# Gated linear attention feeding a two-layer MLP: time order inside the chunks, and scores by halves in two column tiles

## The chip, the cores and the metric

The kernel runs on one core of a Trainium2 chip. The time is the device time of one execution in microseconds. The kernel before was run three times: 701.5, 701.19 and 699.17 us, a median of 701.19.

## What is computed

An attention block with complex decays (a running state per head, and no softmax) is followed by an MLP with a squared ReLU. B is 4, H 8, S 768 and D 48, all in f32; the MLP is 384 x 2048 x 384 over 3072 tokens.

```python
mag = sqrt(a_re**2 + a_im**2)
a = (a_re + 1j*a_im) * minimum(mag, 0.999) / (mag + 1e-6)
for t in range(S):                       # state: complex D x D for each batch and head
    state = a[t][:, None] * state + outer(k[t], v[t])
    y[t] = q[t] @ real(state)
x = y.transpose(0, 2, 1, 3).reshape(B*S, H*D)      # 3072 x 384
out = maximum(x @ w_in, 0)**2 @ w_out              # 384 -> 2048 -> 384
```

## The kernel before

**Units.** The work is cut into 6 units of 512 time steps (rows of the 3072 tokens). A unit is 4 chunks of 128 steps. The 8 heads form two halves z of 4 heads and four pairs i of two heads; pairs 0 and 1 belong to z = 0. The decays become a running product P, so that y = (q P) against (k / P): with the real and imaginary parts side by side, a head's queries and keys are 96 long, and inside a chunk the output is the masked product of scores with v, plus what the state from earlier chunks gives.

**Steps of a unit.** `load` brings a, q, k and v. `chain` normalises the decays on ACT and DVE, multiplies them up (`inner`, over 4 neighbouring steps; `totals` and `scan` over the rest, with PE transposes of `xn` there and `back` again), and `apply` makes the queries and keys: L1156 and L1160 are the products and sums with the running product, L1167 to L1179 the inverse, L1190 the products with q and k. `gather` (L1226) copies the keys by DMA from `f` into `KC`, where partitions are time. Then come the pairs:

- `turn` (units 2 to 5) brings queries and keys into `QT`, with partitions over the 96: two 32 x 32 block transposes of DVE (L1262) and 12 DMAs. `turn_pe` (units 0 and 1) does it by 16 PE transposes a pair (L1285) and 4 ACT copies (L1289).
- `score` (L1303), once per head: keys against queries for 4 chunks, 128 x 128 each, into a PSUM bank `sc`. DVE multiplies the bank by the causal mask (L1306) into `A`, which stands in SBUF.
- `keep` (L1331): keys against v, which DVE adds up into the states after each chunk (L1340, L1342, in `St` and `S`).
- `mix`: for each chunk and both heads v against `A` (L1355), and the state against the queries (L1359), into `yp`; the first head lands on partitions 0 to 47, the second on 64 to 111. ACT copies `yp` to `yt` (L1365), and DMAs bring it to `xT` (L1373), the MLP's input.

`dense` is the MLP, twice a unit on 256 rows: the first layer (L1395), ReLU and square on ACT (L1426, L1427), and the second: plain in unit 0 (L1441), and in units 1 to 5 by blocks of 128 x 192 (L1492), mostly 7 products in place of 8, with sums on DVE (L1507, L1516). Early in the kernel DVE also converts the weights to the layouts that the MLP reads (`convert`, L812 to L819).

**Who sets the order.** Every step is recorded in a `Plan` with its engine, an estimated duration, the keys that it reads and writes, and a rank. `Plan.order` then plays the program through: it takes the engine that can start soonest and gives it the ready step of the lowest rank. The instructions are written out in that order, and each engine runs its own in order, waiting by semaphores. On PE a step with `slack=True` that is fed by DMA is placed as if its input came 2.0 us later, any other that another engine feeds 0.6 later. `Plan.order` walks a Python set of engine names, so ties can fall differently from one build to the next: the profiled build and the rows printed here differ in units 0 and 1 in this way, with the same instructions.

**Where time lies.** Inside a chunk, time step 4t + c stands at partition 32c + t: `v`, `KC`, the columns of `QT`, the scores and the mask are in this order, and the copy L1365 puts the time back in order, writing to `yt` with elements 16 bytes apart. Sums of complex products are one operation on both parts, for which the imaginary factor is kept a second time with its sign changed (`minus`, L1044, and a third plane of `e`, `el`).

Of the kernel before, what the change touches and what calls it, by code (L numbers as in the profile page):

```python
# [598 lines left out]
def fast_path(ctx, tc, q, k, v, a_re, a_im, moe_w_in, moe_w_out, out, flag):  # L599
# [38 lines left out]
    def sb(name, n, dtype=F32, rows=C):  # L638
        return const.tile([rows, n], dtype, name=name)
# [33 lines left out]
    mask = sb("mask", C)  # L673
# [12 lines left out]
            for n in ("d0", "d1", "d2", "sc0", "sc1", "tr0", "tr1", "yp")}  # L686
# [40 lines left out]
    SUM = 0.22  # L727
    checked = []
# [28 lines left out]
    def two(t):  # L757
# [9 lines left out]
    tkeys = [[("QT", 2)], [("QT", 2), ("A", 2)], [("v", 1)]]  # L767
# [4 lines left out]
            (QT[0].bitcast(U32)[:, 0:2 * PW], [("QT", 0)]),  # L772
            (QT[1].bitcast(U32)[:, 0:2 * PW], [("QT", 1)]),
# [81 lines left out]

    def load(n):
# [23 lines left out]
        for i in range(W):  # L880
            b, s = divmod(n * L + i * C, S)
            src = v[b, :, s:s + C, :].rearrange("h (t c) d -> c t h d", c=W)
            for c in range(W):
                vrank = (CHAIN, 1) if n == 1 else (DENSE, 6 + n)
                dma(pool, [("xT", (n - (vs(n) == vs(n - 1))) % 2, NM - 1)] if n else [("gate",)], [("v", vs(n))],
                    lambda i=i, c=c, src=src: pool.dma_start(  # L886
                        out=t[32 * c:32 * c + 32, i], in_=src[c]), vrank, 32 * 1536, 4.0,
                    group=n)

    def chain(n):  # L890
# [57 lines left out]
        def inner(z):  # L948
# [4 lines left out]

            for c in range(1, W):
# [6 lines left out]
                for r, op in ((0, ALU.subtract), (1, ALU.add)):  # L961
                    step("DVE", tt(m // 2), [("in", z, 0), ("in", z, 1)] + key(z, 0), [("a", z)],
                         lambda c=c, r=r, op=op: dve.tensor_tensor(  # L963
                             out=a[:, r, :, c], in0=f[0][:, r], in1=f[1][:, 1 - r], op=op), ahead)
            xh = xn.rearrange("p r (h d) -> p r h d", h=H)[:, :, ts(z, HH)]
            step("ACT", ac(Z // W), [("a", z)], [("xn", 0, z), ("xn", 1, z)],
                 lambda: act.copy(out=xh[:, 0:2], in_=a[:, :, :, W - 1]), ahead)  # L967
# [716 lines left out]
```

## Time and profile before

| | |
|---|---|
| median of 3 runs (lowest, highest) | 701.19 us (699.17, 701.5) |
| the profiled execution | 698.23 us |
| its span, from the first to the last instruction | 696.4 us |
| granted TensorE clock over the span | 0.998 |
| PE busy, matmul instructions | 625.9 us, 4058 |
| DVE, ACT, POOL busy | 545.3, 351.5, 178.0 us |
| moved by DMA | 79.51 MB |

The span is one execution under the hardware profiler, and the profiled execution's time is 1.8 us longer than it. PE is the matrix engine, PEld its weight loads, DVE, ACT and POOL the vector, scalar and GpSimd engines, SP an engine that issues DMAs; an engine's row with a q behind its name is its queue. A row of a group reads: line, engine, operation, out <- in (partitions x elements), count | busy us, mean ns of one | idle us before it, and what ended it. An f32 matmul instruction of a 128 x 128 weight shows up as two passes on PE, so passes are counted in the timeline and source instructions in the order. The lengths in PE's rows overlap, and some passes are missing from the records.

### The profile page before, as it was taken

To read this page: it belongs to the slowest core of one execution; us is meant where nothing else is said; L and a number is where in the kernel's file an instruction comes from. 1 tells how busy PE (TensorE), PEld (TensorE's weight loads), DVE (VectorE), ACT (ScalarE), POOL (GpSimd) and SP (SyncE) were. 2 spreads that over 40 slices of the span, in tenths; PEclk is the share of its full clock that TensorE was granted. 3 is DMA by queue.
4 is the path that set the end of the run, shared out by engine and by line. 5 is a ranking of instruction groups with operands and counts; after the bars stand their busy time and mean duration, and the time that the engine had idled before them with its cause. 6 is when DMAs were issued, how large, how long until landed. Compare 5 with 4: busy or idle time off the path is not lost.

```text
span 696.4 us, 11428 instructions
## 1 busy us (share of the span) xinstructions
PE 625.9 (90%) x4058; PEld 563.6 (81%) x4058; DVE 545.3 (78%) x1111; ACT 351.5 (50%) x580; POOL 178.0 (26%) x334
## 2 busy tenths in 40 slices
PE   0115999999979999999999999999999999999996
PEld 0004887686768999998999998989999989989995
DVE  6999994889897699486898796999788988338631
ACT  6687738865864254346453437363456361142230
POOL 6604461143300005105036041043050033023100
PEclk9999999999999999999999999999999999999999
DMA  9751469021630005644018571027560025368600
GB/s 282 233 208 45 113 138 295 9 61 36 167 106 12 12 13 132 172 114 129 13 38 213 139 158 34 1 69 200 130 163 10 24 72 130 95 243 298 229 2 27
DMA packets 56354, 79.51 MB, mean 114 GB/s; under 512 B 10944, under 2 KB 38464, under 8 KB 56288
## 3 DMA queue, kind: packets, MB, share of 16 engines
q0 software_dynamic: 15232, 40.72, 19.2%
q1 hardware_dynamic: 36928, 32.98, 18.4%
q10 hardware_dynamic: 4128, 4.98, 2.8%
q8 instruction: 34, 0.56, 0.4%
q14 instruction: 32, 0.26, 0.1%
HBM read 48.76 MB, written 4.72 MB: 77 GB/s over the span
## 4 chain that ended last, share of the span: by engine, by line
PE 83%; DVE 11%; DMA 2%; issue 1%; SPq 1%; ACT 1%; DVEq 0%; ACTq 0%
PE d L1395 33%; PE d L1492 27%; PE d L1441 6%; PE sc L1303 5%; PE tr L1331 3%; PE yp L1355 3%; PE yp L1359 2%; PE tr L1395 1%; PE sc L1395 1%; DVE f L957 1%; DMA aq<-in_a_im_dram 1%; DVE f L1190 1%; PE tr L985 1%; DVE f L1156 1%; DVE aq L963 1%
## 5 line engine op out<-in xcount | busy, mean ns | idle before, releaser
L1395 PE MATMUL d<-xT,w 128*128 128x256 f32 x1056 | 233.6, 380 | 0.4 <-DMA xT<-yt 0.4
L1395 PEld LDWEIGHTS d<-xT,w 128*128 128x128 f32 x1056 | 199.1, 190 | 27.8 <-issue 1.2
L1492 PE MATMUL d<-w,g 128*128 128x192 f32 x832 | 143.3, 327 | 0.0
L1492 PEld LDWEIGHTS d<-w,g 128*128 128x128 f32 x832 | 135.5, 190 | 0.7 <-issue 0.4
L1426 ACT ACTIVATE g<-d 128x512 f32<-128x512 f32 x88 | 52.5, 596 | 117.0 <-PE d L1395 103.3
L1226 POOL DMA_DIRECT2D KC<-f x160 | 78.9, 501 | 93.7 <-DVE f L1190 49.5
L1453 POOL DMA_DIRECT2D out_dram<-ot x22 | 12.4, 565 | 268.4 <-DVE ot L1516 228.1
L1427 ACT ACTIVATE g<-g 128x512 f32<-128x512 f32 x96 | 60.6, 631 | 3.1
L1365 ACT COPY yt<-yp 112x512 f32<-112x512 f32 x24 | 26.3, 1095 | 70.0 <-PE yp L1359 70.0
L886 POOL DMA_DIRECT2D v<-in_v_dram x80 | 47.8, 605 | 50.2 <-issue 36.5
L1507 DVE TENSOR_TENSOR g<-g 128x512 f32<-128x512 f32 x56 | 37.8, 685 | 28.7 <-ACT g L1427 21.3
L1492 PE MATMUL d<-T,g 128*128 128x192 f32 x336 | 59.9, 327 | 0.0
L1492 PEld LDWEIGHTS d<-T,g 128*128 128x128 f32 x336 | 54.9, 190 | 0.6 <-issue 0.6
L1303 PE MATMUL sc<-QT 96*128 96x128 f32 x368 | 46.3, 279 | 2.0 <-ACT QT L1289 2.0
L1156 DVE TENSOR_TENSOR f<-aq,xn 128x384 f32<-128x384 f32 (+1 forms) x64 | 45.3, 752 | 2.0 <-ACT xn L1107 2.0
L1303 PEld LDWEIGHTS sc<-QT 96*128 96x128 f32 x368 | 43.2, 192 | 4.0 <-ACT QT L1289 2.4
L1441 PE MATMUL d<-w,g 128*128 128x384 f32 x128 | 42.9, 487 | 0.0
L1306 DVE TENSOR_TENSOR A<-sc,mask 128x512 f32<-128x512 f32 x45 | 30.0, 681 | 14.7 <-PE sc L1303 14.6
L957 DVE TENSOR_TENSOR f<-aq 128x384 f32<-128x384 f32 x72 | 37.0, 553 | 0.7
L1441 PEld LDWEIGHTS d<-w,g 128*128 128x128 f32 x128 | 23.8, 190 | 15.4 <-DVE w L819 1.0
L1516 DVE TENSOR_TENSOR ot<-ot,d 128x192 f32<-128x192 f32 x61 | 20.8, 350 | 18.8 <-PE d L1492 17.5
L985 PE MATMUL tr<-perm,xn 128*128 128x128 f32 x36 | 5.9, 300 | 29.4 <-ACT xn L967 29.4
(180 smaller groups left out, 959.0 us busy)
## 6 DMA issues: line engine op xcount, KB each, us to landing
QT<-aq SPq DMA_DIRECT2D x128, 64.0 KB, 2.2
f<-in_moe_w_in_dram POOLq DMA_DIRECT2D x8, 768.0 KB, 7.0
f<-in_moe_w_out_dram POOLq DMA_DIRECT2D x8, 768.0 KB, 6.8
KC<-f POOLq DMA_DIRECT2D x104, 48.0 KB, 2.2
out_dram<-ot POOLq DMA_DIRECT2D x22, 192.0 KB, 2.3
QT<-aq ACTq DMA_DIRECT2D x64, 64.0 KB, 2.2
v<-in_v_dram POOLq DMA_DIRECT2D x80, 48.0 KB, 3.4
xT<-yt SPq DMA_DIRECT2D x36, 96.0 KB, 2.5
```

The costliest lines, as they stand in the source:

```text
L886: lambda i=i, c=c, src=src: pool.dma_start(out=t[32 * c:32 * c + 32, i], in_=src[c]), vrank, 32 * 1536, 4.0,
L957: lambda c=c, j=j: dve.tensor_tensor(out=f[j], in0=a[:, :, :, c - 1], in1=a[:, j, :, c].unsqueeze(1).to_broadcast([C, 2, HH, D]), op=ALU.m ...
L1156: lambda j=j, r=r: dve.tensor_tensor(out=f4[:, j, r], in0=a[:, r], in1=over(j), op=ALU.mult), late[z])
L1226: lambda i=i, c=c, queue=queue: queue.dma_start(out=kc[32 * c:32 * c + 32, i], in_=nat[32 * i:32 * i + 32, c]),
L1303: pe.matmul(sa[:, j], lhsT=T[:, j, 1, h], rhs=T[:, j, 0, h], start=True, stop=True)
L1306: step("DVE", tt(L) + 0.05, [(b,)], [("A", a)], lambda: dve.tensor_tensor(out=As[a].rearrange("p (j t) -> p j t", j=W), in0=sa, in1=mask4, ...
L1395: pe.matmul(ps, lhsT=w1[:, f // FP, m, ts(f % FP, C)], rhs=xT[:, n % 2, m, ts(grp, G)], start=(m == 0), stop=(m == NM - 1))
L1426: act.activation(out=o, in_=ps, func=AF.Relu)
L1427: act.activation(out=o, in_=o, func=AF.Square)
L1441: pe.matmul(ps, lhsT=gt[:, f % 2, ts(i, C)], rhs=w2[:, f], start=(f == 0), stop=(f == NF - 1))
L1492: pe.matmul(bank[b][:, 0:DH], lhsT=g4[:, r, j], rhs=w(j), start=first and j == 0, stop=last and j == NT - 1)
L1507: step("DVE", tt(4 * C), gk(x0, h) + gk(x1, h), gk(o, h), lambda: dve.tensor_tensor(out=g4[:, o, sl], in0=g4[:, x0, sl], in1=g4[:, x1, sl] ...
```

## The change

Inside a chunk, time now stands in order at the partitions: step t at partition t in even chunks. In odd chunks the two halves of 64 are exchanged (`places`): step 64 + t at partition t, and step t at partition 64 + t. `v` and `KC` are loaded so, with one or two DMAs a chunk instead of four. The scores of a chunk come in two matmuls: the keys of the first half against all 128 queries, and the keys of the second half against its own 64 queries alone, each 64 rows of `sc`, at partition 0 or 64. For chunks j and j + 1 the first half goes to partitions 0 and 64, then the second half to 64 and 0. What no matmul writes is zeroed once at the start. The mask is two chunks wide, 256 columns.

The columns of `QT` are in time order too: DVE's and PE's transposes now write their elements 16 bytes apart, and L1365 becomes a plain copy. A key of `QT` stands for one head instead of both, and the PE transposes are grouped by head and part instead of by c.

The planes with changed sign go; in the scan a complex sum is two operations, a difference and a sum, on half the elements each. The last inner product writes `xn` directly, and ACT copies it back into `a` later, at a lower rank. Of the state sums those without an earlier state become ACT copies, and each chunk's has its own key. Not shown: the copies of `e` and `el` that go, and `apply`, where the same three steps after the exponential multiply k in first (L1176) and correct the inverse last (L1180), with keys of their own.

```diff
-    mask = sb("mask", C)
+    mask = sb("mask", 2 * C)
...
+    CH = C // 2
     pool.memset(mask, 1.0)
-    for c in range(W):
-        rows = mask[32 * c:32 * c + 32]
-        pool.affine_select(out=rows.rearrange("p (c t) -> p c t", c=W),
-                           in_=rows.rearrange("p (c t) -> p c t", c=W),
-                           pattern=[[1, W], [W, 32]], compare_op=ALU.is_ge, fill=0.0,
-                           base=-c, channel_multiplier=-W)
-    mask4 = mask.unsqueeze(1).to_broadcast([C, W, C])
+    for o in range(2):
+        for p0 in (0, CH):
+            part = mask[p0:p0 + CH, ts(o, C)]
+            pool.affine_select(out=part, in_=part, pattern=[[1, C]], compare_op=ALU.is_ge,
+                               fill=0.0, base=-(p0 ^ (CH * o)), channel_multiplier=-1)
+    mask4 = mask.rearrange("p (o t) -> p o t", o=2).unsqueeze(1).to_broadcast([C, W // 2, 2, C])
     dve.memset(ypair, 0.0)
+    for b in ("sc0", "sc1"):
+        dve.memset(bank[b], 0.0)
...
+    SCORE = 0.7
...
+    def places(i):
+        return [(CH, 0, CH), (0, CH, CH)] if i % 2 else [(0, 0, C)]
...
-            src = v[b, :, s:s + C, :].rearrange("h (t c) d -> c t h d", c=W)
-            for c in range(W):
+            src = v[b, :, s:s + C, :].rearrange("h t d -> t h d")
+            for p0, t0, m in places(i):
                 vrank = (CHAIN, 1) if n == 1 else (DENSE, 6 + n)
                 dma(pool, [("xT", (n - (vs(n) == vs(n - 1))) % 2, NM - 1)] if n else [("gate",)], [("v", vs(n))],
-                    lambda i=i, c=c, src=src: pool.dma_start(
-                        out=t[32 * c:32 * c + 32, i], in_=src[c]), vrank, 32 * 1536, 4.0,
+                    lambda i=i, p0=p0, t0=t0, m=m, src=src: pool.dma_start(
+                        out=t[p0:p0 + m, i], in_=src[t0:t0 + m]), vrank, m * 1536, 4.0,
                     group=n)
...
-                    step("DVE", tt(m // 2), [("in", z, 0), ("in", z, 1)] + key(z, 0), [("a", z)],
-                         lambda c=c, r=r, op=op: dve.tensor_tensor(
-                             out=a[:, r, :, c], in0=f[0][:, r], in1=f[1][:, 1 - r], op=op), ahead)
-            xh = xn.rearrange("p r (h d) -> p r h d", h=H)[:, :, ts(z, HH)]
-            step("ACT", ac(Z // W), [("a", z)], [("xn", 0, z), ("xn", 1, z)],
-                 lambda: act.copy(out=xh[:, 0:2], in_=a[:, :, :, W - 1]), ahead)
+                    end = c == W - 1
+                    step("DVE", tt(m // 2), [("in", z, 0), ("in", z, 1)] + key(z, 0),
+                         [("xn", r, z)] if end else [("a", z)],
+                         lambda r=r, op=op, o=xh[:, r] if end else a[:, r, :, c]: dve.tensor_tensor(
+                             out=o, in0=f[0][:, r], in1=f[1][:, 1 - r], op=op), ahead)
+            step("ACT", ac(Z // W), [("xn", 0, z), ("xn", 1, z)], [("a", z)],
+                 lambda: act.copy(out=a[:, :, :, W - 1], in_=xh), (CHAIN, n + 0.05))
...
-            step("DVE", tt(cnt), [(own, 0), (own, 1)], writes,
-                 lambda: dve.tensor_tensor(out=dst, in0=g1, in1=g2, op=ALU.add), rk)
-
-        def minus(t, lo=None, hi=None, view=None):
-            im = t[:, 1] if view is None else view[:, 1, :, lo:hi]
-            ni = t[:, 2] if view is None else view[:, 2, :, lo:hi]
-            dve.tensor_scalar(out=ni, in0=im, scalar1=-1.0, scalar2=None, op0=ALU.mult)
-
-        E = [("e", 0), ("e", 1), ("e", 2)]
+            for r, op in ((0, ALU.subtract), (1, ALU.add)):
+                step("DVE", tt(cnt // 2), [(own, 0), (own, 1)], writes,
+                     lambda r=r, op=op: dve.tensor_tensor(
+                         out=dst[:, r], in0=g1[:, r], in1=g2[:, r], op=op), rk)
...
-            step("DVE", 0.12, I, I, lambda: minus(inc), ahead)
...
-                queue = sp if n < EARLY and c % 2 else pool
+            for p0, t0, m in places(i):
+                queue = sp if n < EARLY and i % 2 else pool
+                t0, m4 = 32 * i + t0 // W, m // W
                 dma(queue, keys, [(k_, z, q_) for q_ in range(p, p + np)
                                   for k_ in ("KC", "KC%d" % (i == 3))],
-                    lambda i=i, c=c, queue=queue: queue.dma_start(
-                        out=kc[32 * c:32 * c + 32, i], in_=nat[32 * i:32 * i + 32, c]),
-                    rank, 32 * w * 4, group=(n, p))
+                    lambda i=i, p0=p0, t0=t0, m=m, m4=m4, queue=queue: queue.dma_start(
+                        out=kc[p0:p0 + m, i], in_=nat[t0:t0 + m4]),
+                    rank, m * w * 4, group=(n, p))
...
-                dst = T6[:, i % 2].rearrange("p j (k h c t) -> p k c h j t", k=2, h=2, c=W)
+                dst = T6[:, i % 2].rearrange("p j (k h t c) -> p k c h j t", k=2, h=2, c=W)
...
-                ps = bank[b][0:R].rearrange("p (k t) -> p k t", k=4)
-
-                def go(c=c, ps=ps):
-                    for j in range(2):
-                        for h in range(2):
-                            pe.transpose(ps[:, 2 * j + h], nat[:, j, c, h], ident)
-                step("PE", 0.46, [("f", z, 2 * (i % 2) + j) for j in range(2)], [(b,)],
-                     go, rank)
-                dst = QT[s].rearrange("p (i k c t) -> p c i k t", i=W, k=4, c=W)[0:R, c]
-                step("ACT", ac(512), [(b,)], [("QT", s)], lambda ps=ps, dst=dst: act.copy(
-                    out=dst, in_=ps.rearrange("p k (i t) -> p i k t", i=W)), rank,
-                    group=(n, i))
+            for h in range(2):
+                for j in (1, 0):
+                    b = "d%d" % take("d", 3) if n == 0 else trs[take("tr", 2)]
+                    ps = bank[b][0:R].rearrange("p (t c) -> p c t", c=W)
+
+                    def go(h=h, j=j, ps=ps):
+                        for c in range(W):
+                            pe.transpose(ps[:, c], nat[:, j, c, h], ident)
+                    step("PE", 0.46, [("f", z, 2 * (i % 2) + j)], [(b,)], go, rank)
+                    dst = QT[s].rearrange("p (i k t) -> p k i t", i=W, k=4)[0:R, 2 * j + h]
+                    step("ACT", ac(512), [(b,)], [("QT", s, h)], lambda b=b, dst=dst: act.copy(
+                        out=dst, in_=bank[b][0:R].rearrange("p (i t) -> p i t", i=W)), rank,
+                        group=(n, i))
...
-                for j in range(W):
-                    pe.matmul(sa[:, j], lhsT=T[:, j, 1, h], rhs=T[:, j, 0, h],
-                              start=True, stop=True)
-            step("PE", 0.9, [("QT", s)], [(b,)], go, rank, slack=True)
+                for j0 in range(0, W, 2):
+                    for half in range(2):
+                        for j in (j0, j0 + 1):
+                            p0, t0 = CH * (half ^ (j % 2)), CH * half
+                            pe.matmul(sa[p0:p0 + CH, j, t0:C], lhsT=T[:, j, 1, h, t0:t0 + CH],
+                                      rhs=T[:, j, 0, h, t0:C], start=True, stop=True)
+            step("PE", SCORE, [("QT", s, h)], [(b,)], go, rank, slack=True)
             step("DVE", tt(L) + 0.05, [(b,)], [("A", a)], lambda: dve.tensor_tensor(
-                out=As[a].rearrange("p (j t) -> p j t", j=W), in0=sa, in1=mask4,
+                out=As[a].rearrange("p (j o t) -> p j o t", o=2, t=C),
+                in0=bank[b].rearrange("p (j o t) -> p j o t", o=2, t=C), in1=mask4,
                 op=ALU.mult), rank)
...
-                def go2(js=js, ps=ps):
-                    for j in js:
-                        o = new if j == 3 else at[j + 1]
-                        if at[j] is None:
-                            dve.tensor_copy(out=o, in_=ps[:, j])
-                        else:
-                            dve.tensor_tensor(out=o, in0=ps[:, j], in1=at[j], op=ALU.add)
-                step("DVE", len(js) * (tt(2 * D) + 0.04),
-                     [(b,), ("S", n % 2, i)] + ([("St", s)] if last else []),
-                     [("S", (n + 1) % 2, i)] if last else [("St", s)], go2, rank)
+                for j in js:
+                    o = new if j == 3 else at[j + 1]
+                    reads = [(b,)] + ([("S", n % 2, i)] if j == 0 else [("st", s, j)])
+                    writes = [("S", (n + 1) % 2, i)] if j == 3 else [("st", s, j + 1)]
+                    if at[j] is None:
+                        step("ACT", ac(2 * D), reads, writes, lambda o=o, j=j, ps=ps: act.copy(
+                            out=o, in_=ps[:, j]), rank)
+                    else:
+                        step("DVE", tt(2 * D) + 0.04, reads, writes,
+                             lambda o=o, j=j, ps=ps: dve.tensor_tensor(
+                                 out=o, in0=ps[:, j], in1=at[j], op=ALU.add), rank)
...
-            step("ACT", ac(L) + 0.5, [("yp",)], [("yt", y)], lambda: act.copy(
-                out=yts[y][0:64 + D].rearrange("p (j t c) -> p j c t", j=W, c=W),
-                in_=ypair[0:64 + D].rearrange("p (j c t) -> p j c t", j=W, c=W)), rank)
+            step("ACT", ac(L), [("yp",)], [("yt", y)], lambda: act.copy(
+                out=yts[y][0:64 + D], in_=ypair[0:64 + D]), rank)
```

On PE, in unit 2, these rows stand where the first pair's scores are (`sc` from `QT`), between the MLP's second layer (`d` from `w_67`), the keep (`tr`) and the mix (`yp`); a row's count is of source instructions. Before:

```order
L1492 MATMUL d_110<-w_67,g 128x192 x4
L1492 MATMUL d_112<-w_67,g 128x192 x4
L1331 MATMUL tr_115<-v_77,KC_75 96x48 x6
L1331 MATMUL tr_116<-v_77,KC_75 96x48 x6
L1303 MATMUL sc_113<-QT_73 128x128 x4
L1303 MATMUL sc_114<-QT_73 128x128 x4
L1492 MATMUL d_110<-w_67,g 128x192 x4
L1492 MATMUL d_111<-w_67,g 128x192 x4
L1355 MATMUL yp<-A_86,v_77 48x128
L1355 MATMUL yp<-A_87,v_77 48x128
```

Now, with 64 x 128 and 64 x 64 outputs:

```order
L1400 MATMUL d_111<-xT,w_66 128x256 x3
L1497 MATMUL d_112<-w_67,g 128x192 x4
L1497 MATMUL d_110<-w_67,g 128x192 x4
L1305 MATMUL sc_113<-QT_73 64x128 x2
L1305 MATMUL sc_113<-QT_73 64x64 x2
L1305 MATMUL sc_113<-QT_73 64x128 x2
L1305 MATMUL sc_113<-QT_73 64x64 x2
L1305 MATMUL sc_114<-QT_73 64x128 x2
L1305 MATMUL sc_114<-QT_73 64x64 x2
L1305 MATMUL sc_114<-QT_73 64x128 x2
L1305 MATMUL sc_114<-QT_73 64x64 x2
L1497 MATMUL d_112<-w_67,g 128x192 x4
```

The two heads' scores, 8 instructions then and 16 now, stand between two runs of the second layer in both; the keep has moved ahead of this place, and behind it the mix follows two runs later in both.

On DVE, in unit 0, these rows end with the key and query products of the last pair (`f_71` from `aq_69`, L1190, now L1189). `A` from `sc` are the masks, `St` and `S` from `tr` the state sums, `w_66` the weights' conversion. Before:

```order
L1306 TENSOR_TENSOR A_86<-sc_113,mask 128x512
L1306 TENSOR_TENSOR A_87<-sc_114,mask 128x512
L1174 TENSOR_SCALAR f_71<-f_71,lv 128x384
L1340 COPY St_89<-tr_115 96x96
L1342 TENSOR_TENSOR St_89<-tr_115,St_89 96x96 x2
L1176 TENSOR_SCALAR f_71<-f_71 128x384
L1342 TENSOR_TENSOR S_85<-tr_116,St_89 96x96
L1179 TENSOR_SCALAR f_71<-f_71,lv,aq_69 128x384
L1190 TENSOR_TENSOR f_71<-f_71,aq_69 128x2x4x48 x2
L1190 TENSOR_TENSOR f_71<-aq_69 128x2x4x48 x2
```

Now:

```order
L815 TENSOR_SCALAR w_66<-g 128x768
L819 TENSOR_SCALAR w_66<-g,w_66 128x768
L1348 TENSOR_TENSOR St_88<-tr_115,St_88 96x96
L1308 TENSOR_TENSOR A_86<-sc_113,mask 128x512
L1348 TENSOR_TENSOR St_88<-tr_115,St_88 96x96
L1308 TENSOR_TENSOR A_87<-sc_114,mask 128x512
L1348 TENSOR_TENSOR S_85<-tr_116,St_88 96x96
L1172 TENSOR_SCALAR f_71<-f_71,lv 128x384
L1176 TENSOR_SCALAR f_71<-f_71,lv,aq_69 128x384
L1180 TENSOR_SCALAR f_71<-f_71 128x384
L1189 TENSOR_TENSOR f_71<-f_71,aq_69 128x2x4x48 x2
L1189 TENSOR_TENSOR f_71<-aq_69 128x2x4x48 x2
```

Before, the masks and state sums in front of the last pair's products are those of the second pair; now the second pair's stand further up and these are the third pair's, behind two steps of the weights' conversion, and the last pair's products come after all of them.

More of the change, by code (lines that the diff above doesn't have):

```diff
@@ L1001, in totals @@
                 out=e[:, j], in_=p4), ahead)
-            if j == 1:
-                step("ACT", ac(DM), [b], [("e", 2)], lambda: act.mul(
-                    out=e[:, 2], in_=p4, mul=-1.0), ahead)
             if not ends:
@@ L1007, in totals @@
                     out=el[:, j], in_=last), ahead)
-                if j == 1:
-                    step("ACT", ac(NM), [b], [("el", 2)], lambda: act.mul(
-                        out=el[:, 2], in_=last, mul=-1.0), ahead)
             def start():
@@ L1064, in scan @@
                  ahead)
-            step("DVE", 0.09, I, I, lambda: minus(top), ahead)
             span = 4 if cross else 8
@@ L1093, in scan @@
                          out=xn[:, r].rearrange("p (g x w) -> p w x g", x=4, w=4),
[L1094 removed]
+                         in0=own[0], in1=own[1], op=ALU.add if r else ALU.subtract), ahead)
             if not ends:
```

49 lines of the change are left out of this document (25 added, 24 removed).

## The prediction

> **What bounds the kernel now.** I read the page's head and chain first, then the busy times by stretch, then TensorE's timeline around a score and a mix, and last the groups by shape.
>
> ```profile
> span 696.4 us, 11428 instructions
> PE 625.9 (90%) x4058; PEld 563.6 (81%) x4058; DVE 545.3 (78%) x1111; ACT 351.5 (50%) x580; POOL 178.0 (26%) x334
> PE 83%; DVE 11%; DMA 2%; issue 1%; SPq 1%; ACT 1%; DVEq 0%; ACTq 0%
> ```
>
> TensorE (PE) is the bound, with VectorE (DVE) holding the chain for 11%. The stretches show where (columns: stretch, its length, then busy time and instructions of PE, PEld, DVE, ACT, POOL; granted clock, DMA).
>
> ```profile
> 9.00:47.50 38.50, 3.52 (x12) 2.11 (x12) 36.83 (x92) 30.92 (x48) 18.92 (x29) 1.00 0.82 273
> 47.50:90.00 42.50, 27.49 (x277) 25.52 (x277) 41.64 (x91) 32.23 (x51) 15.99 (x32) 1.00 0.29 70
> 90.00:170.00 80.00, 79.97 (x344) 59.61 (x343) 64.84 (x143) 51.42 (x88) 27.42 (x45) 1.00 0.42 111
> 170.00:210.00 40.00, 35.64 (x318) 29.52 (x317) 35.62 (x69) 28.76 (x52) 10.06 (x21) 1.00 0.45 127
> 210.00:600.00 390.00, 390.00 (x2588) 364.34 (x2587) 319.74 (x636) 182.51 (x305) 86.87 (x166) 1.00 0.36 91
> 609.00:616.00 7.00, 6.58 (x37) 5.53 (x33) 0.35 (x1) 1.23 (x2) 2.12 (x4) 1.00 0.19 56
> ```
>
> Until 90 us DVE is the bound (36.83 of 38.50, 41.64 of 42.50): unit 0's chain and the weights. From 90 on PE never rests, but for 4.36 us in unit 1's pairs (170 to 210) and 0.42 us at the last xT. So a us taken off PE after 90, or off DVE's way to the first dense product, is a us off the end; nothing else is, unless it becomes late.
>
> **The change, part by part.**
>
> Scores. In the timeline, starts matter, not lengths, since matmuls overlap.
>
> ```profile
> 295.11 1.95 PE L1303 MATMUL sc<-QT 96*128 96x128 f32 x16
> 296.89 2.77 PE L1492 MATMUL d<-w,g 128*128 128x192 f32 x16
> ...
> 303.38 2.77 PE L1492 MATMUL d<-w,g 128*128 128x192 f32 x16
> 306.07 0.43 PE L1355 MATMUL yp<-A,v 128*48 128x128 f32 x4
> 306.33 0.39 PE L1359 MATMUL yp<-QT,S 96*48 96x128 f32 x4
> 306.55 0.39 PE L1355 MATMUL yp<-A,v 128*48 128x128 f32 x4
> ...
> 307.65 0.39 PE L1359 MATMUL yp<-QT,St 96*48 96x128 f32 x4
> 307.97 4.17 PE L1492 MATMUL d<-w,g 128*128 128x192 f32 x24
> 311.97 0.38 PE L1395 MATMUL d<-xT,w 128*128 128x256 f32 x1
> ```
>
> Two heads' scores, 16 passes (an f32 matmul is two), take 296.89 - 295.11 = 1.78 us: 0.89 a head, 0.111 a pass of 128 columns. The mix already uses two column tiles (heads at partitions 0 and 64), and its four passes start 0.22 us apart (306.33 to 306.55), which is 0.055 a pass: the tiles run side by side. A head's new scores are twice (two tiles x 128 columns, then two tiles x 64). The first is the mix's 0.22. No row has a 64-column pass; the nearest is the keep's.
>
> ```profile
> L1331 PE MATMUL tr<-v,KC 128*96 128x48 f32 x272 | 26.6, 246 | 1.6 <-DMA KC<-f 1.6
> 632.22 18.20 PE d L1492 x112
> ```
>
> Its 48 columns cost 26.6 / 272 = 0.098 with a 96-column weight; half of 0.22 is the lower end (0.11 for the group of four), no gain at all over 128 columns the upper (0.22). I take 0.13, nearer the lower, because the weights are 64 columns and the two tiles load side by side in the mix. A head then costs 2 x (0.22 + 0.13) = 0.70 (ends 0.66 and 0.88). PE is the bound for 40 of the 48 (units 1 to 5): 40 x 0.19 = **-7.6** (ends -9.2 and -0.4).
>
> Going into column tiles and out again. A dense pass costs 18.20 / 112 = 0.1625, so the 16 from 303.38 end at 305.98; the mix starts at 306.07 (+0.09), its first group takes 0.26 (+0.04), its last, from 307.65, leaves at 307.87 and the dense follows at 307.97 (+0.10); the 24 passes from there should reach 311.87 and reach 311.97 (+0.10). So 0.33 us per visit. The old scores are full width and pay none. Before, PE makes 24 visits, 20 of them in units 1 to 5; the new order has 46, of which 37 there, since most scores stand apart from a mix. 17 x 0.33 = **+5.6**; below nothing is excluded, as a switch takes no work away. Three quarters of the score gain is gone here.
>
> The start. DVE loses the negations, two copies become direct writes, and each complex sum becomes two half sums; the waits on ACT's copy into xn go.
>
> ```profile
> L967 ACT COPY xn<-aq 128x384 f32<-128x384 f32 x12 | 6.1, 505 | 6.7 <-DVE aq L963 6.6
> L1044 DVE TENSOR_SCALAR yt<-yt 128x96 f32<-128x96 f32 x12 | 2.5, 211 | 0.3
> L1306 DVE TENSOR_TENSOR A<-sc,mask 128x512 f32<-128x512 f32 x45 | 30.0, 681 | 14.7 <-PE sc L1303 14.6
> L919 DVE TENSOR_TENSOR f<-f 128x768 f32<-128x768 f32 x12 | 11.5, 956 | 6.8 <-ACT f L916 6.6
> ```
>
> The copy gives 0.5 of latency; six negations in unit 0 give about 0.9 (0.21 for the two long ones), of which the halves take 0.4 back; and two weight steps fewer stand ahead of the scan, of which I count 0.7: the pairs start some 1.7 us earlier. But the new DVE order puts two more masks (30.0 / 45 = 0.67 each), three more keep sums for two copies (+0.3) and four weight or unit-1 steps like L919 (0.9) ahead of pair 3's products: +5.2, so those end about 3 us later. What they feed is quicker: the gather of keys.
>
> ```profile
> 79.28 1.14 SPq L1226 DMA_DIRECT2D KC<-f  x2
> 80.51 1.80 SPq L1373 DMA_DIRECT2D xT<-yt  x3
> 82.36 5.02 SPq L1226 DMA_DIRECT2D KC<-f  x6
> 85.51 1.82 DMA KC<-f
> ```
>
> Eight issues on SP, with three xT transfers among them, held pair 3's keys from 79.28 to 87.33; now it is four issues (2.4 at the 0.6 of these rows) with none among them and a landing of 1.8: 4.2 instead of 8.1. With this, and the last two masks no later than before by DVE's sum, the last mix comes 1.5 us sooner: **-1.5** (ends -3 and +1.5, if DVE waits for a score in its new order).
>
> Unit 1. Scores wait for one head's half of QT alone, the key gather is a third of the issues (four for twelve), four St copies go to ACT: of the 4.36 us of rest I take **-1.0** (ends -4.4 and +3).
>
> The last xT.
>
> ```profile
> 609.43 1.09 ACT yt L1365
> L1365 ACT COPY yt<-yp 112x512 f32<-112x512 f32 x24 | 26.3, 1095 | 70.0 <-PE yp L1359 70.0
> L1426 ACT ACTIVATE g<-d 128x512 f32<-128x512 f32 x88 | 52.5, 596 | 117.0 <-PE d L1395 103.3 <-DMA QT<-aq 11.0 <-DVE aq L1262 2.3
> ```
>
> The yt copy no longer spreads its elements 16 bytes apart, and should cost what a plain 512 costs: 0.5 less, and PE's 0.42 of rest goes: **-0.4**. The other 23 copies have cover already.
>
> The spread itself has moved: DVE's transposes (units 2 to 5) now write 16 bytes apart, PE's (units 0 and 1) into PSUM likewise.
>
> ```profile
> L1262 DVE STREAM_TRANSPOSE aq<-f 128x768 f32<-128x768 f32 x32 | 29.5, 954 | 0.2
> L1087 DVE TENSOR_TENSOR KC<-e,yt 128x384 f32<-128x384 f32 x24 | 12.4, 550 | 0.0
> L1092 DVE TENSOR_TENSOR xn<-KC 128x384 f32<-128x384 f32 x12 | 9.7, 812 | 0.3
> L1285 PE MATMUL tr<-ident,f 128*96 128x128 f32 x64 | 9.0, 277 | 2.6 <-ACT QT L1289 1.6 <-DVE St L1340 1.0
> ```
>
> L1092 writes spread (64 bytes apart) and costs 0.26 more than L1087 on 384; at that rate a transpose of 768 takes 0.52 longer, at the ACT copy's 0.75, at best nothing: up to 32 x 0.52 = 17 us of DVE, under 70 us of DVE rest from 210 to 600. On the path lie the two transposes ahead of a unit's first scores, 1.0 to 1.5 a unit; the planner leaves 2.0 of slack there and 0.6 ahead of a mix. I take **+1.0** (ends 0 and +6). POOL's fewer issues, ACT's copies of St and xn and the other finer waits have cover: zero, and at most the ends above.
>
> Sum: -7.6 + 5.6 - 1.5 - 1.0 - 0.4 + 1.0 = -3.9. The profiled execution took 698.23, 3 us under the median of 701.19, and the runs spread over 2.3; I put the -3.9 on the median: **697.3**.
>
> **The rivals.**
>
> A, the tiles do not run side by side in this order: successive matmuls go to tiles 0, 64, 64, 0, where the mix alternates, and 64-column passes come twice as fast as any in the trace. A head then costs 0.88 (groups at 0.22 throughout) to 0.99 (only neighbours in different tiles overlap): the first term is -0.4 to +4.0, the sum +3.3 to +7.7, the time 704.5 to 709. It decides from 0.81 a head on. Against it: the mix's 0.055 a pass. [...] Chance 0.15.
>
> B, slower: the spread writes end on the path. PE's transposes have no cover in units 0 and 1: 64 passes of 9.0 / 64 = 0.14 in unit 1 (0.109 where they follow one another, 7.0 in all); at the 1.84 of the yt copy against the plain one, +6; pair 3 of unit 0 +1.5; DVE's lateness 1.5 a unit instead of 1.0 in all, +5. Sum -3.9 + 12.5 = +8.6, time 710; half of it, 703.5. It decides when the passes of L1285 exceed 0.17. For it speaks the ACT copy; against it that no PE row shows a spread write. [...] Chance 0.20.
>
> C, the waits go wholly: unit 1's rest -4.4, start -3, a head at 0.66, transposes free: 697.3 - 3.4 - 1.5 - 1.6 - 1.0 = 689.8. Chance 0.15.
>
> The shapes 64x128 and 64x64 stand in the new order, so that the change is not made is left at 0.02.
>
> **How the numbers follow.** My forecast has 0.48, with a range of its own from 693 to 701. A measurement tells about 0.3% here, 2.1 us: faster is under 699.1, slower over 703.3. Faster: 0.38 of the forecast, all of C, 0.02 of B: 0.55. Same: 0.09, with 0.02 of A and 0.03 of B: 0.14. Slower: 0.01, 0.13, 0.15 and the rest: 0.31. The range takes in C's end and half of A and B: 691 to 706.5.
>
> **What would show it.** 16 passes of 64x128 and 64x64 per head starting 0.70 apart; 37 visits of 0.33 after 90 us; PE's stretch 210 to 600 still without rest; PE steady from about 88.5; L1262 at 0.95 to 1.7 without PE waiting for a mask; L1285 at 0.109. A head over 0.81, L1285 over 0.17 or PE waiting for masks in units 2 to 5 would make it wrong.

## The result, and the profile after

The changed kernel takes 706.77 us, the median of 5 runs (705.58 to 708.47); the kernel before took 701.5 (699.17 to 704.48, 5 runs). The ratio is 1.0073, with a 95% interval of 1.0044 to 1.0103: slower by 0.7%, where 697.3 was forecast and 706.5 was the upper end. The profiled execution took 706.77, its span is 705.0.

The head of its page and its chain:

```profile
span 705.0 us, 11855 instructions
PE 630.2 (89%) x4442; PEld 559.2 (79%) x4442; DVE 557.3 (79%) x1125; ACT 339.5 (48%) x586; POOL 96.3 (14%) x166
PE 61%; DVE 26%; DMA 6%; ACT 3%; issue 2%; SPq 1%; ACTq 0%; DVEq 0%
```

PE's share of the chain fell from 83% to 61%, and DVE's rose from 11% to 26%. The stretches, with the columns of the prediction's:

```profile
47.50:90.00 42.50, 31.36 (x373) 27.54 (x373) 41.65 (x83) 32.47 (x53) 5.07 (x9) 1.00 0.31 71
90.00:170.00 80.00, 76.12 (x303) 56.07 (x302) 62.36 (x145) 50.09 (x85) 14.28 (x21) 0.98 0.41 108
170.00:210.00 40.00, 39.18 (x394) 30.30 (x393) 32.58 (x62) 28.47 (x56) 4.32 (x8) 1.00 0.48 131
210.00:600.00 390.00, 380.84 (x2739) 350.99 (x2739) 332.70 (x644) 174.12 (x307) 40.32 (x68) 0.99 0.37 90
```

PE rests 3.88 us between 90 and 170, where it rested 0.03, and 9.16 between 210 and 600, where it did not rest. In unit 1 (170 to 210) its rest fell from 4.36 to 0.82. The granted clock is under 1.00 in the two stretches with the rests. What PE waited for, from 90 to 210 (first row, its longest wait there) and from 210 on (total us, times, longest us):

```profile
PE d L1446 <- DVE w L822: 3.1, 1, 3.1
```

```profile
PE yp L1359 <- DVE A L1308: 3.0, 4, 1.6
PE d L1400 <- DMA xT<-yt: 2.9, 1, 2.9
PE tr L1334 <- ACT St L1344: 2.6, 2, 1.7
PE sc L1305 <- DMA QT<-aq: 0.3, 1, 0.3
```

The scores themselves did what the forecast said. In the timeline of PE two heads' scores follow a mix without leaving the column tiles:

```profile
281.43 0.39 PE L1363 MATMUL yp<-QT,St 96*48 96x128 f32 x4
281.65 1.50 PE L1305 MATMUL sc<-QT 96*64 96x128 f32 x32
283.08 1.08 PE L1497 MATMUL d<-w,g 128*128 128x192 f32 x5
```

From 281.65 to 283.08 are 1.43 us; less the 0.10 for leaving, 0.665 a head. The groups by shape show where DVE's time went:

```profile
L1262 DVE STREAM_TRANSPOSE aq<-f 128x768 f32<-128x768 f32 x32 | 47.5, 1573 | 0.3
L1285 PE MATMUL tr<-ident,f 128*96 128x128 f32 x64 | 8.5, 276 | 0.8 <-ACT QT L1288 0.8
L1371 ACT COPY yt<-yp 112x512 f32<-112x512 f32 x24 | 13.9, 581 | 63.1 <-PE yp L1363 55.7 <-DVE aq L1262 7.4
```

A DVE transpose takes 1.573 instead of 0.954, the ACT copy 0.581 instead of 1.095, and PE's transposes, which spread in PSUM now, 8.5 / 64 = 0.133 a pass instead of 0.141.

**An account of the spans** (705.0 - 696.4 = +8.6), by the starts of the last passes of the last mix of units 0, 1 and 5, which are at 92.5, 209.4 and 609.1 before and at 89.7, 208.7 and 615.3 after. Up to the first: -2.8. To the second: +2.1, made of the wait for w_out (3.1, and by the spacing of PE's starts 1.8 more for the passes at half rate, a granted clock of 0.50, behind it), unit 1's rest (-3.5), its scores (8 x -0.22) and 8 more visits to column tiles (8 x 0.33), which is +2.3. From there to the end: +9.3, made of waits (9.2), passes at half rate behind the wait for xT and one for St (1.6 each, 3.2), 32 heads' scores (-7.1), 9 more visits (+3.0) and the last xT (-0.4): +7.9, so that 1.4 is not accounted for.

### The profile page after: what moved, and what is told of

It reads as the page before. It is cut to its first block, busy times and chain, and to the rows that moved or that the text cites. A ratio compares the mean times of both kernels' runs of the same rounds, so it can differ in the third digit from the quotient of the medians.

```text
span 705.0 us, 11855 instructions
## 1 busy us (share of the span) xinstructions
PE 630.2 (89%) x4442; PEld 559.2 (79%) x4442; DVE 557.3 (79%) x1125; ACT 339.5 (48%) x586; POOL 96.3 (14%) x166
## 4 chain that ended last, share of the span: by engine, by line
PE 61%; DVE 26%; DMA 6%; ACT 3%; issue 2%; SPq 1%; ACTq 0%; DVEq 0%
PE d L1400 21%; PE d L1497 20%; PE d L1446 5%; DVE aq L1262 4%; PE sc L1305 4%; DVE f L1189 3%; DMA aq<-in_q_dram 3%; DVE f L1151 3%; PE yp L1359 3%; PE tr L1334 2%; PE yp L1363 2%; DVE g L1512 2%; DVE aq L1155 2%; DVE KC L1038 1%; DMA QT<-aq 1%
## 5 line engine op out<-in xcount | busy, mean ns | idle before, releaser
L1400 PE MATMUL d<-xT,w 128*128 128x256 f32 x1056 | 237.7, 382 | 2.9 <-DMA xT<-yt 2.9
L1400 PEld LDWEIGHTS d<-xT,w 128*128 128x128 f32 x1056 | 199.6, 191 | 30.6 <-DMA xT<-yt 3.3
L1226 POOL DMA_DIRECT2D KC<-f x52 | 27.6, 545 | 174.9 <-DVE f L1189 125.3
L1446 PE MATMUL d<-w,g 128*128 128x384 f32 x128 | 45.5, 505 | 3.1 <-DVE w L822 3.1
L1262 DVE STREAM_TRANSPOSE aq<-f 128x768 f32<-128x768 f32 x32 | 47.5, 1573 | 0.3
L1371 ACT COPY yt<-yp 112x512 f32<-112x512 f32 x24 | 13.9, 581 | 63.1 <-PE yp L1363 55.7
L1446 PEld LDWEIGHTS d<-w,g 128*128 128x128 f32 x128 | 24.4, 197 | 18.7 <-DVE w L822 3.7
L1305 PEld LDWEIGHTS sc<-QT 96*64 96x64 f32 x736 | 34.1, 137 | 5.6 <-issue 3.3
L1305 PE MATMUL sc<-QT 96*64 96x128 f32 (+1 forms) x736 | 37.4, 250 | 0.6 <-DMA QT<-aq 0.3
L1359 PE MATMUL yp<-A,v 128*48 128x128 f32 x320 | 32.4, 277 | 3.5 <-DVE A L1308 3.3
```

What stands on the lines that cost most here:

```text
L1262: lambda nat=nat, dst=dst, j=j: dve.transpose(out=dst[:, j], in_=nat), rank)
L1305: pe.matmul(sa[p0:p0 + CH, j, t0:C], lhsT=T[:, j, 1, h, t0:t0 + CH], rhs=T[:, j, 0, h, t0:C], start=True, stop=True)
L1359: pe.matmul(ypair[64 * h:64 * h + D, ts(j, C)], lhsT=v5[:, j, 2 * i + h], rhs=aa[h][:, j], start=True, stop=at[j] is None)
L1400: pe.matmul(ps, lhsT=w1[:, f // FP, m, ts(f % FP, C)], rhs=xT[:, n % 2, m, ts(grp, G)], start=(m == 0), stop=(m == NM - 1))
L1446: pe.matmul(ps, lhsT=gt[:, f % 2, ts(i, C)], rhs=w2[:, f], start=(f == 0), stop=(f == NF - 1))
```

## The experiments

Runs 1 to 6 keep, on every engine, the order of the kernel they are made from; 7 and 8 have an order of their own, and part 9 keeps that of 8. All have the ties of the plan fixed as in the profiled builds (DVE first), unless said otherwise. Ratios are to the kernel before as it was built beside each; what ties do to those builds comes last.

**1. DVE's transposes write contiguously again** (units 2 to 5 then compute with columns in another order).

```diff
-dst = T6[:, i % 2].rearrange("p j (k h t c) -> p k c h j t", k=2, h=2, c=W)
+dst = T6[:, i % 2].rearrange("p j (k h c t) -> p k c h j t", k=2, h=2, c=W)
```

> The changed kernel in the same order on every engine; only DVE's two transposes per pair in units 2 to 5 write contiguously again (L1262), so that the columns of QT are not in time order there and the numbers of those units mean nothing. Theory 1, DVE: the spread write made each of the 32 transposes 0.62 us longer (1.573 against 0.954), DVE fell behind, and PE waited behind it in units 3 to 5. Then L1262 is back at about 0.95, and PE's waits for A (3.0), St (2.6) and QT (0.3) with the slow clock after the longest of them (1.6) go: some 7.5 us less than the changed kernel, about 699; the wait for xT in unit 2 (2.9) stays. Theory 2, queues and order: the waits come from the new order (St copies on ACT, xT) and the earlier loads; then at most 2 us go, 705 or more.

Measured: 697.22, ratio 0.9899 (0.9863 to 0.9936). Its groups and PE's waits from 210 on:

```profile
L1262 DVE STREAM_TRANSPOSE aq<-f 128x768 f32<-128x768 f32 x32 | 29.2, 952 | 0.3
```

```profile
PE d L1400 <- issue: 2.4, 1, 2.4
PE sc L1305 <- DMA QT<-aq: 0.8, 1, 0.8
```

The waits for A and St are gone, and nothing else was touched; the wait for xT in unit 2 stays (it is the row with "issue"), and so does the one for QT, which was expected to go. Theory 1 holds: 0.0126 less than the changed kernel with the same ties (1.0025, below), some 8.9 us, for the 7.5 expected.

**2. The same lines the other way round, in the kernel before.**

> The kernel before in the same order on every engine; only its DVE transposes in units 2 to 5 write with elements 16 bytes apart (the columns of QT are then in another order than the rest takes them to be, so the numbers of those units mean nothing). Theory 1: L1262 goes from 0.954 to about 1.57, 32 x 0.62 = 20 us more of DVE, of which the order before hides some by its slack of 2.0; PE waits for masks and keys in units 2 to 5: slower by 3 to 9 us. Theory 2: 70 us of DVE rest hide it, within 1 us of the kernel before.

Measured: 715.66, ratio 1.0149 (1.0082 to 1.0216); the kernel before with the same ties has 0.9926 (below), so it costs 2.2%, some 15 us, over the 9 of theory 1. The profile is of its longest run, 723.8 us, so only its waits from 210 on are read; the longest are of the kinds that the changed kernel has, in an order that had none of them:

```profile
PE yp L1355 <- DVE A L1306: 6.5, 8, 1.6
PE tr L1331 <- DVE S L1342: 1.7, 1, 1.7
```

So the spread write alone, without tiles or finer keys, makes PE wait.

**3. v by 32 partitions, 16 issues a unit.**

```diff
-... pool.dma_start(out=t[p0:p0 + m, i], in_=src[t0:t0 + m]) ...
+... [pool.dma_start(out=t[p0 + x:p0 + x + 32, i], in_=src[t0 + x:t0 + x + 32]) for x in range(0, m, 32)] ...
```

> The changed kernel in the same order; only each load of v is issued by 32 partitions, 16 DMAs a unit as before instead of 6. Theory 1: POOL, done with v after 4.65 us instead of 10.56, started the loads of w_out 8.7 us earlier (93.95 against 102.61), these ran against the loads of unit 2's a and q, ACT waited 5.07 us at L922 with a weight conversion queued behind, and PE waited 3.1 us for the converted w_out and ran 8 passes at half speed (2.0 us). With 16 issues again that goes: 5 us less than the changed kernel, about 702. Theory 2: the loads of a and q were late for their own sake (SP's order puts q first); no change, 706 to 707.

Measured: 697.78, ratio 0.9935 (0.9910 to 0.9960). The timeline of POOL and ACT in the changed kernel, first, and in the kernel before show what was suspected:

```profile
89.31 4.65 POOL L892 DMA_DIRECT2D v<-in_v_dram  x6 [6.00 <-issue]
93.95 1.44 POOL L795 DMA_DIRECT2D QT<-in_moe_w_out_dram  x2
...
115.34 1.48 ACT L922 ACTIVATE f<-aq 128x1536 f32<-128x1536 f32 x1 [5.07 <-DMA aq<-in_q_dram]
```

```profile
92.06 10.56 POOL L886 DMA_DIRECT2D v<-in_v_dram  x16 [8.60 <-issue]
102.61 1.46 POOL L792 DMA_DIRECT2D QT<-in_moe_w_out_dram  x2
...
111.41 1.49 ACT L916 ACTIVATE f<-aq 128x1536 f32<-128x1536 f32 x1
```

And the DMA issues from 88 to 116 (KB each, median us to landing), of the changed kernel and of this run:

```profile
aq<-in_a_im_dram SPq DMA_DIRECT2D x2, 192.0 KB, 18.0
```

```profile
aq<-in_a_im_dram SPq DMA_DIRECT2D x2, 192.0 KB, 6.3
```

With POOL freed sooner, w_out was requested 8.7 us earlier than in the kernel before; the loads of a's imaginary parts for the next unit took 18.0 us to land, where run 3's took 6.3; ACT stood at L922, and the conversion of w_out behind it came late for PE. With 16 issues the wait at L1446 is gone from PE's list, though the transposes still spread. Theory 1 holds: 0.0090 of the changed kernel's 1.0025, some 6 us, for the 5 expected. Not all of it need be w_out's: the wait for xT in unit 2 is 1.3 here instead of 2.9, and no wait has passes at half rate behind it (the granted clock is 1.00 in its stretches from 90 to 600). The edit also makes v's own transfers smaller; they landed in 4.6 to 4.8 us by six and in 5.4 by sixteen, so that v itself was not late, but no run holds their size fixed and moves the request of w_out alone.

**4. Both repairs.**

> The changed kernel in its order, with both repairs that gained alone: contiguous transposes of DVE in units 2 to 5 (numbers there mean nothing) and v issued by 32 partitions. Theory (two separate causes): the gains add, 0.990 + 0.9935 against 1.0073: 0.976 to 0.979 of the kernel before, 686 to 689 where that takes 703.8. Rival (one lateness, seen twice): the second repair gives little, 0.985 to 0.99.

Measured: 690.74, ratio 0.9835 (0.9777 to 0.9893). Against the changed kernel with the same ties (1.0025, below) the single repairs gave 0.0126 and 0.0090, both together 0.0190: most of their sum of 0.0216. It is a smaller gain than the 0.976 to 0.979 expected, and the interval reaches into the rival's 0.985 to 0.990 too, so the ratio alone does not decide. The traces do. Run 1 keeps the wait for w_out (first row), run 3 keeps those for A and St (3.3 and 2.6), and here all of them are gone; the longest wait after 90 is the one for xT (second row):

```profile
PE d L1446 <- DVE w L822: 3.5, 1, 3.5
```

```profile
PE d L1400 <- DMA xT<-yt: 1.7, 1, 1.7
```

So there are two causes.

**5. Contiguous transposes and scores at full width.**

```diff
-pe.matmul(sa[p0:p0 + CH, j, t0:C], lhsT=T[:, j, 1, h, t0:t0 + CH], rhs=T[:, j, 0, h, t0:C], ...)
+pe.matmul(sa[:, j], lhsT=T[:, j, 1, h], rhs=T[:, j, 0, h], ...)
...
```

Not shown: the loops around it, and the exchange of halves in `places` and in the mask, which goes.

> As the run with contiguous transposes, and in the same order, but scores at full width: one matmul of 128 x 128 a chunk, no exchange of halves in odd chunks, a mask without exchange. Theory 1 (the halves gain what was forecast): PE's scores cost 0.89 a head instead of 0.665 (40 x 0.22 = 8.9 more in units 1 to 5) and 17 visits to column tiles fewer (5.6 less): 3.3 us above the run with halves, less where PE has waits that take it up. Rival A (no gain from two tiles): equal to it or up to 5 us below.

Measured: 700.36, ratio 0.9957 (0.9926 to 0.9988), 3.1 us over run 1 by the medians, where 3.3 was expected; the intervals overlap, so the size is less sure than its sign. Rival A falls by the 0.665 a head: two tiles do run side by side. The visits leave about a third of that gain.

**6. ACT's QT issues given to POOL** (on top of 3). The trace of run 3 had shown this at one of the waits for St, first DVE, then ACT:

```profile
482.34 2.95 DVE L1262 STREAM_TRANSPOSE aq<-f 128x768 f32<-128x768 f32 x2
```

```profile
482.52 3.33 ACTq L1267 DMA_DIRECT2D QT<-aq  x4
486.81 0.23 ACT L1344 COPY St<-tr 96x96 f32<-96x96 f32 x1 [3.72 <-DVE St L1348]
```

```diff
-... queue.dma_start(...
+... (pool if j == 2 else sp).dma_start(...
```

> The changed kernel in its order with v issued by 32 partitions, and the third of the QT DMAs that ACT issues is issued by POOL at the same place of the plan; DVE's transposes still write spread. Theory A: PE's waits for St in unit 4 (2.6 with 1.6 of slow clock) come from ACT, where the St copies stand behind QT issues that wait for late transposes; they go, and the yt copies come sooner: 3 to 5 us less than the run with v by 32 partitions (697.8). Theory B: DVE alone sets it, since the issues would wait wherever they stand: within 1.5 us of it, with PE's waits for masks (3.6) still there.

Measured: 696.07, ratio 0.9877 (0.9831 to 0.9923), under run 3 by 1.7 us by the medians and by 4 by the ratios, whose intervals overlap: the time does not tell the theories apart. PE's waits from 210 on:

```profile
PE yp L1359 <- DVE A L1308: 3.4, 5, 1.6
PE d L1400 <- issue: 1.7, 1, 1.7
PE tr L1334 <- ACT St L1344: 1.3, 1, 1.3
```

Half of the wait for St goes (1.3 for 2.6), the masks' stays (3.4 for 3.3): the ACT queue passes DVE's lateness on, and the masks' part does not come from it.

**7. The plan is told the transposes' true time.**

```diff
-step("DVE", tt(768), ...)
+step("DVE", 1.5 if j else 1.5, ...)
```

> The changed kernel with one number: the plan is told that a transpose takes 1.5 us instead of 0.87. The order in units 2 to 5 changes (42 visits to column tiles on PE instead of 46); the loads of v and w_out in unit 0 stay as in the changed kernel. Theory A (the plan did not know that DVE would be late, and PE had other work): PE's waits behind DVE go, 4 to 7 us less than the changed kernel, ratio 0.997 to 1.002. Theory B (the work itself is too much for DVE ahead of the pairs): the waits only change place, ratio within 0.003 of the changed kernel's 1.007.

Measured: 704.42, ratio 1.0012 (0.9990 to 1.0034); with the same ties the changed kernel has 1.0025, so nothing that can be told. PE's waits from 210 on:

```profile
PE d L1400 <- issue: 3.9, 1, 3.9
PE yp L1359 <- DVE A L1308: 1.2, 6, 0.2
PE tr L1334 <- ACT St L1344: 1.2, 1, 1.2
PE sc L1305 <- DMA QT<-aq: 1.1, 1, 1.1
PE d L1400 <- DMA xT<-yt: 1.0, 1, 1.0
```

In all they stayed as long (8.4, where the changed kernel has 8.8), but not by kind: those for A, St and QT fell from 5.9 to 3.5, and those of L1400, for xT as far as the rows say (the one with "issue" stands where the changed kernel waits for xT in unit 2), rose from 2.9 to 4.9. Theory A's 0.997 to 1.002 was met, but by the ties. Telling the plan shortened DVE's part of the waits and gained no time; that the work is too much for DVE at these places, as B has it, is not shown by this run.

**8. Only the keys in time order**, as the weights of the two halves need it; queries, columns of scores and outputs are in the old order, and a half's queries are four runs of 16 columns. Unlike runs 1, 2, 4 and 5 it computes what the kernel should. Edits 3 and 6 are in it (POOL's issues are in the plan too), and the plan is told 1.5 us for the keys' transposes. Not shown: the mask, the PE transposes and the yt copy, which follow the old order.

```diff
+dst = T6[:, i % 2].rearrange("p j (k h t c) -> p k c h j t" if j else "p j (k h c t) -> p k c h j t", k=2, h=2, c=W)
...
+o4, q4 = [x.rearrange("p (c t) -> p c t", c=W)[:, :, 16 * half:32] for x in (sa[p0:p0 + CH, j], T[:, j, 0, h])]
+pe.matmul(o4, lhsT=T[:, j, 1, h, t0:t0 + CH], rhs=q4, start=True, stop=True)
```

> A version with the right numbers: keys in time order (spread, 1.5 us in the plan), queries, scores' columns and outputs in the old column order (contiguous, 0.87; the second half's queries are then 4 runs of 16 columns, and the yt copy writes spread again), v issued by 32 partitions, the third of the QT DMAs on POOL instead of ACT. 16 transposes lose 0.62 us each: 10 us of DVE. If DVE's lateness and the loads of w_out were the two causes, it comes to 0.978 to 0.985 of the kernel before. If runs of 16 columns slow the scores' passes, PE's score rows show it (0.665 a head in the changed kernel), and it stays over 0.985.

Measured: 689.94, ratio 0.9789 (0.9740 to 0.9838). The groups, the stretch from 210 to 600, and a pair's scores:

```profile
L1262 DVE STREAM_TRANSPOSE aq<-f 128x768 f32<-128x768 f32 x32 | 38.2, 1272 | 0.2
```

```profile
210.00:600.00 390.00, 389.63 (x2907) 360.01 (x2906) 327.55 (x647) 183.91 (x308) 86.66 (x162) 1.00 0.36 92
```

```profile
282.02 1.51 PE L1306 MATMUL sc<-QT 96*64 96x128 f32 x32
283.45 2.87 PE L1498 MATMUL d<-w,g 128*128 128x192 f32 x16
```

PE is without rest again but for 0.37 us, and the scores take the same 1.43 from runs of 16 columns. It has the lowest ratio of all runs here, though its interval overlaps that of run 4, and it is 1.4% under the kernel before at equal ties (0.9789 to 0.9926). Both causes were expected to bring it to 0.978 to 0.985.

**9. That version with full scores, and with 6 issues for v.**

With full scores:

> The version with only the keys in time order, in the same order on every engine, but scores at full width (one matmul of 128 x 128 a chunk, chunks not exchanged). If the halves pay what the rows say (0.89 against 0.665 a head, less 0.33 a visit to column tiles): 3 to 4 us over the version with halves, 0.983 to 0.985 against 0.979 of the kernel before. If most of the gain is DVE's and POOL's, and visits eat the halves: equal within 1.5 us.

With 6 issues:

> The same version with v in 6 DMAs a unit again instead of 16. If the early loads of w_out are a cause of their own, also in this version: PE waits some 3 us for the converted w_out at 118 to 122 us and runs slowly after it, 4 to 8 us over the version with 16 (0.979), so 0.985 to 0.990. If it was particular to the changed kernel's order: 0.977 to 0.981.

Measured: 690.91, ratio 0.9840 (0.9789 to 0.9890), and 691.92, ratio 0.9838 (0.9768 to 0.9908). The first is where it was expected, the second a little under; neither is told from 0.9789 by its interval. The profiles say more. Between the last mix of unit 0 and the end lie 596.3 us with halves and 599.0 with full scores (690.0 - 93.7, 689.1 - 90.1), so 2.7 for the halves. With 6 issues PE waits 1.8 us for the converted w_out, which the version with 16 does not: the cause is there too. Whether it is smaller, this profile does not show, since in it unit 0's last mix ends at 93.7 and not at 90 (see the last section), so that PE comes later to this place.

**10. What ties do.**

The kernel before, ties as profiled, and the other way:

> The kernel before with the order of ties fixed as in its profiled build (engines walked as DVE, PE, POOL, SP, ACT). 1.000 within 0.003 if builds matter little; its span's stages on this chip show where the 703.9 of the later runs lies over the 698.2 of the first profile.

> The kernel before with ties fixed the other way (ACT first), which moves instructions in units 0 and 1 only. If the ties explain the spread of the runs of before, it differs from the other by 2 us or more; if not, both agree within 1.5 us.

The changed kernel, the same two:

> The changed kernel with ties fixed as in its profiled build (DVE first). The kernel before took 697.93 so and 702.99 with ties the other way, and its runs mix the two. If the change itself costs what the waits in its trace say (about 13 us in units 2 to 5 and 5 in unit 0, against 3 at the start, 3 in unit 1 and 3 at the scores), this takes 706 to 709, 8 to 11 us over the kernel before with the same ties.

> The changed kernel with ties fixed the other way (ACT first): one step of ACT moves, in unit 0. Within 1.5 us of the run with DVE first. If it is 3 us or more off, what a build makes of ties is as large as the change, and the +5.3 of the result says little.

| ties | before | changed |
|---|---|---|
| DVE first, as profiled | 697.93, 0.9926 (0.9904 to 0.9948) | 704.79, 1.0025 (1.0001 to 1.0050) |
| ACT first | 702.99, 1.0002 (0.9976 to 1.0029) | 706.25, 1.0044 (1.0014 to 1.0073) |

With equal ties the change costs 6.9 us as profiled, a little under what was expected, and 3.3 with the others, where the intervals overlap. The kernel before depends on ties by some 5 us, the changed one by 1.5 or nothing. The first three runs of the kernel before (701.5, 701.19, 699.17), on which the forecast was put, lie between its two.

## Why the prediction was wrong

- **Scores**: right. 0.70 a head was forecast, 0.665 measured; 46 visits at 0.33 came as counted; run 5 shows the net.
- **The start and unit 1**: right in sign, larger in size: -2.8 for -1.5, and 3.5 us of rest less for -1.0. The order on DVE with more ahead of the last pair did no harm here. The gain at the start is that of two single profiles, and at this place two with the same order lie 3.6 us apart (last section): with ACT first the last mix of unit 0 comes at 94.2 where it came at 93.2 before.
- **The last xT and PE's spread in PSUM**: right; the copy is 0.51 shorter, and a pass of L1285, which writes spread into PSUM now, is no longer than before (0.133 us for 0.141). Rival B's first term did not come.
- **The step that failed, first: DVE's transposes at +1.0 (0 to +6).** Their length was forecast well (0.52 more, 0.62 measured). What failed is "up to 32 x 0.52 = 17 us of DVE, under 70 us of DVE rest": rest in a stretch's sum was taken for cover. That rest lies where DVE waits for PE and ACT (the first two rows are its longest such sums from 210 to 600). Ahead of the mask that PE waits for at 382.67, with six of the longer transposes among its steps, DVE is busy 16.79 of 17.0 us (third row):

```profile
DVE g L1512 <- PE d L1497: 7.9, 6, 3.5
DVE f L936 <- ACT f L931: 6.9, 3, 3.1
366.00:383.00 17.00, 15.30 (x119) 13.11 (x120) 16.79 (x21) 6.29 (x12) 3.76 (x8) 1.00 0.77 180
```

  So 20 us of work came out as 8.9 us on the path (run 1 against the changed kernel at equal ties, 0.0126 of 704), 1.6 of it as passes at half rate behind a wait for St. The order's slack of 2.0 and 0.6 did not cover it. Rival B named the mechanism, with a chance of 0.20 and 5 us for it.
- **Second: "POOL's fewer issues ... have cover: zero".** I asked whether anyone waits for POOL, not what POOL does next. Freed, it asked for w_out 8.7 us sooner, against the loads of a and q, and with 16 issues again the kernel is some 6 us quicker (run 3). None of the rivals had it.
- **Third, smaller: the base.** The runs before lie between those of the two ties, so that they may mix builds; by ties the same change measures +6.9 or +3.3.
- **Open: the wait for xT in unit 2**, 2.9 us and 1.6 of passes at half rate behind it, for which the forecast had nothing ("PE's stretch 210 to 600 still without rest"). It is not the transposes': it stays without the spread (2.4, run 1). It is 1.3 with 16 issues of v (run 3) and gone in version 8, but no run singles out what sets it.
- **The rest of the sum** agrees: with both repairs the ratio is 0.9835 against 0.9926 for the kernel before at equal ties, 6.4 us less, by the intervals give or take 4; the forecast without its +1.0 for the transposes is 4.9 less.

## What to carry to other kernels

Idle time of an engine, summed over a stretch, cannot be counted as cover until it is shown to lie ahead of the step that is made longer; look for where that engine is busy end to end before the bound one needs it. Of an engine that is made free sooner ask what its next instruction is, and with which transfers that will share the DMA engines (here a load took 18.0 us to land, and 6.3 in run 3, where that instruction came later). When a scheduler breaks ties by the order of a set, fix that order before comparing anything of a per cent.

## What the runs showed that was not expected

A rest of PE can cost more than itself. After the 2.89 us wait for xT PE goes on at 315.82, after the wait of 1.74 for St at 496.49, and 1.3 to 1.5 us later the granted clock is 0.50 for some 3.4 us; behind the wait of 3.1 for w_out it is so from 122.6 to 126.0. After one of 1.57 for a mask, which ends at 382.67, it stays at 1.00:

```profile
317.20:320.50 3.30, 3.30 (x9) 2.63 (x8) 3.20 (x7) 1.23 (x2) 0.00 (x0) 0.50 1.11 228
498.10:501.40 3.30, 3.30 (x13) 3.30 (x12) 1.48 (x5) 3.23 (x7) 0.00 (x0) 0.50 0.57 135
382.80:386.20 3.40, 3.40 (x64) 3.33 (x63) 3.40 (x5) 0.58 (x1) 0.00 (x0) 1.00 0.91 242
```

The length of the rest does not settle it: in run 3 PE goes on at 487.09 after a wait of 1.75 for St, and the clock stays at 1.00:

```profile
486.90:490.40 3.50, 3.31 (x26) 3.31 (x27) 2.84 (x7) 1.79 (x5) 0.00 (x0) 1.00 0.71 170
490.40:493.90 3.50, 3.50 (x29) 3.27 (x29) 3.00 (x7) 2.14 (x4) 0.00 (x0) 1.00 0.38 90
```

PE's first work of all, in unit 0, starts at half rate, and how long that lasts differs between executions with the same order. The same 12 transposes, in the version with full scores of part 9 and in version 8:

```profile
63.05 1.48 PE L1285 MATMUL d<-ident,f 128*96 128x128 f32 x12
```

```profile
65.06 2.76 PE L1285 MATMUL d<-ident,f 128*96 128x128 f32 x12
```

By the spacing of PE's starts (a transpose takes 0.213 us, and then 0.109) the rate doubled at 59.2 us in the first and only at 69.1 in the second, and the last mix of unit 0 came 3.6 us later; the column of the granted clock says 1.00 in both. Runs 3 and 6, whose kernels differ only later than this place, are unlike here too (a pass of L1285 in unit 0 takes 314 ns in the mean in run 3 and 342 in run 6; it takes 341 in version 8), so 3 to 4 us between single profiles mean nothing here. What sets the rate is not shown by these runs: the clock is 0.50 after rests of 1.74, 2.89 and 3.1 us and 1.00 after rests of 1.57 and 1.75, and from the first transpose of L1285 on the half rate lasts 3 us in the first of the two executions above (56.2 to 59.2) and 13 in the second (56.2 to 69.1).
